# Decode attention of two models on one core: a scheduler that prices tiling switches and issue time, K of B in 32 KB packets, more places for K

## The chip, the cores and the metric

The kernel runs on one core of a Trainium2 chip. The metric is the device time of one execution in microseconds (us), lower is better. Engines in the profile: PE is the matrix engine, PEld its weight loads, DVE the vector engine, ACT the scalar engine, POOL the general engine, SP (SyncE) the one that issues all DMA transfers here; SPq is its queue. Sixteen DMA engines carry each transfer together: each of the 498 transfers of the kernel leaves 16 completion packets of 4 bytes in the trace. A *place* or *slot* is a buffer in the on-chip memory that holds one load. *Landing* is the moment when a load is complete.

## The reference

Two attention layers with given K and V caches, computed side by side; the outputs are joined on the last axis.

```python
# A: B=16 sequences, 32 new tokens each, D=1024, 32 query heads, 4 K/V heads, 1024 cached positions, head size 128
# B: the same, but with 32 K/V heads
q = (x @ wq).reshape(B, Sq, 32, 128).transpose(0, 2, 1, 3)
scores = einsum("bhqd,bhkd->bhqk", q, k) * 128 ** -0.5      # k, v of A repeated 8 times over heads
p = softmax(scores)
o = einsum("bhqk,bhkd->bhqd", p, v)
out = o.transpose(0, 2, 1, 3).reshape(B, Sq, 4096) @ wo
# result: concatenate([out_A, out_B], axis=-1), everything in bf16
```

B's caches are eight times A's: K and V of B are 268 MB of the 338 MB that the kernel reads. There is little arithmetic per byte, so the transfers matter most.

## The kernel before

The program is written as a list of operations, each with the buffers that it reads and writes. A list scheduler with a small time model then fixes the order of the instructions on each engine, and semaphore waits are derived from the buffers. The work is cut into 128 steps. A step of B handles four heads of one sequence: 1 MB of K, 1 MB of V.

```python
NVB_SLOTS = 3          # places for V of B
NKB_SLOTS = 2          # places for K of B
SP_AHEAD = 1.5         # how far SyncE's issues may run ahead of the modelled DMA stream, us
PE_MODE = {"scoresB": 2, "PVB": 1}
MODE_SWITCH = 0.11     # one price for each change of PE's tiling
...
QB_sb = sb("QB_sb", [P, 3, 4, NTOK], BF)           # Q of B, three places
KB_sb = sb("KB_sb", [P, NKB, 2, 16 * Dh], BF)      # K of B as it is loaded
ost = sb("ost", [P, 2, D], BF)                     # staging of the output
...
# scheduler: an issue on SyncE costs 0.06 us, a transfer its bytes / 390 GB/s, then 1.8 us to landing
free[op.eng] = st + 0.06
xs = max(st + 0.06, dma_free[0])
dma_free[0] = xs + op.dur / dma_bw
op.t1 = dma_free[0] + dma_lat
...
# most loads: 32 reads of one contiguous stretch, each written over four partitions
def wide_load(e, dst, src, groups=32):
    inst = mybir.InstDMACopy(..., ins=e.lower_ap_dma(src.rearrange("(g n) d -> g (n d)", g=groups)), outs=e.lower_ap_dma(dst))
...
# K of B: 128 partitions of 8 KB each, an ordinary load: 128 packets of 8 KB
ksrc = pb["k"][q.b, q.h0:q.h0 + 4].rearrange("a (p s) d -> (a p) (s d)", s=32)
e.dma_start(KB_sb[:, sl, :, :].rearrange("p i n -> p (i n)"), ksrc)
...
# a step of B
st_ktrB(q, 0); st_ktrB(q, 1)              # DVE transposes K in 32 x 32 blocks; the place is free after it
if t + NKB < NIT: st_dmaK(quadsB[t + NKB])
if t >= 1 and t - 1 + NVB < NIT: st_dmaV(quadsB[t - 1 + NVB])
st_scores(q); st_exp(q); st_ptr(q); st_pev(q, "act"); st_pv(q); st_recip(q); st_norm(q, "dve"); st_otr(q, "act")
```

## Time and profile before

| | before |
|---|---|
| time, median of the first 3 runs | 844.96 us (844.0 to 846.38) |
| span of the profiled run | 843.8 us |
| DMA queue of the loads, share of 16 engines | 98.4% |
| PE, DVE, ACT busy | 84%, 66%, 53% |

The first lines of the profile's page of the kernel before, and its DMA part. In the row of tenths each digit is the busy share of one fortieth of the span; GB/s is what moved in it.

```profile
PE 707.7 (84%) x11977; PEld 431.9 (51%) x12104; DVE 553.2 (66%) x1117; ACT 448.3 (53%) x981; POOL 68.1 (8%) x76
...
DMA  9999999999999999999999999999999999999994
GB/s 343 377 412 376 419 418 412 418 421 417 404 415 416 418 420 417 408 403 416 416 419 418 418 419 421 421 405 420 407 409 416 419 419 421 402 404 416 411 405 172
DMA packets 56726, 341.52 MB, mean 405 GB/s; under 512 B 7968, under 2 KB 8480, under 8 KB 17440
...
q1 hardware_dynamic: 56608, 339.77, 98.4%
q8 instruction: 95, 1.56, 0.7%
...
DMA 52%; PE 27%; DVE 15%; SPq 2%; issue 2%; ACT 1%; POOL 1%; DVEq 0%; POOLq 0%
```

Three things say the same: the DMA row is full until the last slice, the load queue (q1) was busy for 98.4% of the span, and over half of the chain that ended last is DMA. q8 are fetches of instructions, which the page counts on the same 16 engines.

What held SyncE's queue before its issues, in the kernel before (who waited, for whom, us in total, times, longest). L825 issues K of B, L514 V of B, L499 everything that goes through the wide load, A's K and V above all.

```profile
SPq L825 <- DVE KBt_sb L859: 139.0, 38, 8.2
SPq L499 <- POOL VAp_sb L834: 82.6, 33, 6.4
SPq L825 <- DVE stat L922: 77.6, 30, 7.5
SPq L825 <- DVE OB_sb L1002: 73.2, 20, 6.3
SPq L514 <- PE ps_o L986: 30.5, 16, 7.9
```

All waits of L825 together are 364 of SyncE's 522 us of waiting. SyncE stands before K of B until DVE has emptied a place.

### The profile page before, as it was taken

The page shows a single profiled execution, that of the slowest core. Times are in us where ns is not written, and L with a number is a line of the kernel's source. Part 1 is how long each engine was busy: PE and PEld are TensorE (multiplying, and loading weights), DVE is VectorE, ACT ScalarE, POOL GpSimd, SP SyncE. Part 2 cuts the span into 40 slices and gives each one's busy share as a digit, 9 for nine tenths or more (in the row PEclk, how much of TensorE's full clock was granted, in tenths as well). Part 3 has the DMA queues.
Part 4 walks back from the last instruction along what each step waited for, and adds up shares of the span by engine and source line. Part 5 has one row for each costly group of instructions (what it writes and reads, how often), then busy time and mean ns, then how long its engine had stood idle before and what let it go on. Part 6 is the DMA issues. An engine that isn't in the chain of part 4 may idle for free.

```text
span 843.8 us, 27217 instructions
## 1 busy us (share of the span) xinstructions
PE 707.7 (84%) x11977; PEld 431.9 (51%) x12104; DVE 553.2 (66%) x1117; ACT 448.3 (53%) x981; POOL 68.1 (8%) x76
## 2 busy tenths in 40 slices
PE   3999999799978798788987879987999867887876
PEld 2555665456545465455554435554565534554543
DVE  0654666566855687567775758774778856757764
ACT  1455666566645465445654545554565634645562
POOL 0000000000001000010000000000000000000000
PEclk9999999999999999999999989999999999999999
DMA  9999999999999999999999999999999999999994
GB/s 343 377 412 376 419 418 412 418 421 417 404 415 416 418 420 417 408 403 416 416 419 418 418 419 421 421 405 420 407 409 416 419 419 421 402 404 416 411 405 172
DMA packets 56726, 341.52 MB, mean 405 GB/s; under 512 B 7968, under 2 KB 8480, under 8 KB 17440
## 3 DMA queue, kind: packets, MB, share of 16 engines
q1 hardware_dynamic: 56608, 339.77, 98.4%
q8 instruction: 95, 1.56, 0.7%
q14 instruction: 23, 0.19, 0.1%
HBM read 337.64 MB, written 2.10 MB: 403 GB/s over the span
## 4 chain that ended last, share of the span: by engine, by line
DMA 52%; PE 27%; DVE 15%; SPq 2%; issue 2%; ACT 1%; POOL 1%; DVEq 0%; POOLq 0%
DMA KB_sb<-in_B_k_cache_dram 33%; DVE KBt_sb L859 12%; PE ps_pj L690 7%; DMA VA_sb<-in_A_v_cache_dram 6%; PE ps_s L894 4%; PE ps_pj L747 4%; DMA VB_sb<-in_B_v_cache_dram 4%; DMA wq_sb<-in_B_wq_dram 3%; PE ps_kt L952 3%; DMA woB_sb<-in_B_wo_dram 2%; PE ps_o L986 2%; DMA wq_sb<-in_A_wq_dram 2%; PE ps_pt L936 2%; PE ps_s L877 2%; DMA acc<-in_B_x_dram 1%
## 5 line engine op out<-in xcount | busy, mean ns | idle before, releaser
L859 DVE STREAM_TRANSPOSE KBt_sb<-KB_sb 128x1024 f32<-128x1024 f32 x256 | 304.9, 1224 | 73.6 <-DMA KB_sb<-in_B_k_cache_dram 64.6
L917 ACT ACTIVATE P_sb<-ps_s 128x512 bf16<-128x512 f32 x256 | 151.4, 597 | 81.4 <-PE ps_s L894 67.7
L909 ACT ACTIVATE PTA_sb<-ps_s 128x1024 bf16<-128x1024 f32 x128 | 131.3, 1026 | 88.1 <-PE ps_s L877 62.2
L894 PE MATMUL ps_s<-KBt_sb,QB_sb 32*32 32x512 bf16 x4096 | 141.5, 383 | 11.8 <-DVE KBt_sb L859 8.8
L620 ACT COPY PT_sb<-ps_pt 128x512 f32<-128x512 f32 x128 | 75.0, 586 | 114.8 <-PE ps_o L986 88.3
L834 POOL COPY VAp_sb<-VA_sb 128x1024 bf16<-128x1024 bf16 x64 | 66.6, 1041 | 758.0 <-DMA VA_sb<-in_A_v_cache_dram 703.7
L690 PE MATMUL ps_pj<-xT_sb,wq_sb 128*128 128x512 bf16 x401 | 112.0, 388 | 12.7 <-DMA wq_sb<-in_B_wq_dram 3.8
L936 PE MATMUL ps_pt<-id,P_sb 128*128 128x128 f32 x512 | 103.1, 303 | 15.2 <-ACT P_sb L917 12.0
L986 PE MATMUL ps_o<-VB_sb,PT_sb 128*32 128x128 bf16 x4096 | 82.0, 223 | 30.3 <-DMA VB_sb<-in_B_v_cache_dram 29.4
L936 PEld LDWEIGHTS ps_pt<-id,P_sb 128*128 128x128 f32 x512 | 81.5, 205 | 40.1 <-ACT P_sb L917 21.7
L986 PEld LDWEIGHTS ps_o<-VB_sb,PT_sb 128*32 128x32 bf16 x4096 | 59.4, 97 | 67.5 <-DMA VB_sb<-in_B_v_cache_dram 44.0
L877 PE MATMUL ps_s<-QT_sb,KTA_sb 128*128 128x256 bf16 x512 | 84.3, 274 | 10.9 <-ACT PTA_sb L909 5.6
L952 PE MATMUL ps_kt<-VAp_sb,PTA_sb 128*128 128x129 bf16 x1024 | 74.3, 220 | 9.0 <-POOL VAp_sb L834 5.3
L894 PEld LDWEIGHTS ps_s<-KBt_sb,QB_sb 32*32 32x32 bf16 x4096 | 48.6, 88 | 64.6 <-DVE KBt_sb L859 14.4
L952 PEld LDWEIGHTS ps_kt<-VAp_sb,PTA_sb 128*128 128x128 bf16 x1024 | 63.4, 97 | 30.4 <-POOL VAp_sb L834 12.3
L1002 DVE TENSOR_SCALAR OB_sb<-ps_o,rinv_all 128x128 bf16<-128x128 f32 x128 | 43.6, 341 | 50.1 <-PE ps_o L986 48.9
L922 DVE TENSOR_TENSOR stat<-stat 64x1 f32<-64x1 f32 x256 | 50.7, 198 | 25.4 <-ACT P_sb L917 17.6
L747 PE MATMUL ps_pj<-woB_sb,OTB_sb 128*128 128x512 bf16 x195 | 56.5, 382 | 8.9 <-DMA woB_sb<-in_B_wo_dram 4.8
L690 PEld LDWEIGHTS ps_pj<-xT_sb,wq_sb 128*128 128x128 bf16 x448 | 41.2, 108 | 43.1 <-DMA wq_sb<-in_B_wq_dram 5.8
L877 PEld LDWEIGHTS ps_s<-QT_sb,KTA_sb 128*128 128x128 bf16 x512 | 44.3, 98 | 36.2 <-ACT PTA_sb L909 10.4
L747 PE MATMUL ps_pj<-woA_sb,OTA_sb 128*128 128x512 bf16 x200 | 54.6, 392 | 7.0 <-DMA woA_sb<-in_A_wo_dram 2.7
L758 DVE TENSOR_TENSOR acc<-acc,ps_pj 128x512 f32<-128x512 f32 x64 | 43.1, 673 | 18.4 <-PE ps_pj L747 17.3
(52 smaller groups left out, 518.8 us busy)
## 6 DMA issues: line engine op xcount, KB each, us to landing
KB_sb<-in_B_k_cache_dram SPq DMA_DIRECT2D x128, 1024.0 KB, 8.7
KA_sb<-in_A_k_cache_dram SPq DMA_DIRECT2D x64, 256.0 KB, 10.1
VA_sb<-in_A_v_cache_dram SPq DMA_DIRECT2D x64, 256.0 KB
wq_sb<-in_B_wq_dram SPq DMA_DIRECT2D x16, 512.0 KB, 11.2
woB_sb<-in_B_wo_dram SPq DMA_DIRECT2D x32, 256.0 KB, 10.2
woA_sb<-in_A_wo_dram SPq DMA_DIRECT2D x32, 256.0 KB, 8.8
wq_sb<-in_A_wq_dram SPq DMA_DIRECT2D x12, 512.0 KB, 11.4
woA_sb<-in_A_wq_dram SPq DMA_DIRECT2D x4, 512.0 KB, 8.9
```

Of the source, the lines that this page charges most:

```text
L620: pr.add("act", lambda e: e.copy(dst_ap, src_ap), reads=reads, writes=writes, name=name + "@act", wtag=wtag, rtag=rtag)
L690: last = e.matmul(ps_pj[:, 0:NTOK], pick(src, j), xT_sb[:, pi, j, :], start=(j == 0), stop=(j == DJ - 1))
L747: last = e.matmul(ps_a[:, 0:OUTW], OT[:, gp, hh, :], wo_[:, hh, oh * OUTW:(oh + 1) * OUTW], start=(hh == 0), stop=(hh == nh - 1))
L834: pr.add("pool", lambda g: g.tensor_copy(VAp_sb[:, sl, :, 0:Dh], VA_sb[:, :, :]), reads=["VA"], writes=[("VAp", sl)], name="VAp_cp", rtag= ...
L859: pr.add("dve", lambda e: e.transpose(KBt_sb[:, sl, t_, :].bitcast(F32).rearrange("p (s r i) -> p s r i", r=2, i=32), KB_sb[:, rs, t_, :]. ...
L877: last = e.matmul(ps_s[:, sbf, c2, i * 2 * P:(i + 1) * 2 * P], KTA_sb[:, sl, c * P:(c + 1) * P], qt, start=True, stop=True)
L894: last = e.matmul(ps_s[32 * cg:32 * cg + 32, sbf, g, :].rearrange("p (sh cl j) -> p sh cl j", sh=4, cl=4), lhsT, kt[32 * a:32 * a + 32, g, ...
L909: pr.add("act", lambda e: e.activation(dst, src, ACTF.Exp, scale=scale), writes=BK_S[sbf] + [("PTA", q.half)], name="expA", rtag={("Sv", s ...
L917: pr.add("act", lambda e, src=src, dst=dst, g=g: e.activation(dst, src, ACTF.Exp, scale=scale, accum_out=st[:, g:g + 1]), writes=[BK_S[sbf ...
L936: last = e.transpose(ps_pt32[:, m * P:(m + 1) * P], p32[:, m:Sk // 2:NPK], id32[:])
L952: last = e.matmul(ps_kt[:, qh * OA0:qh * OA0 + Dh + 1], PTA_sb[:, h, c, qh * P:(qh + 1) * P], VAp_sb[:, sl, 4 * h + c, 0:Dh + 1], start=(h ...
L986: last = e.matmul(ps_o[32 * a:32 * a + 32, 0:Dh], PT_pairs[:, c // 2, 32 * (a ^ (c // 4 * 2)):32 * (a ^ (c // 4 * 2)) + 32, c % 2], VB_sb[ ...
```

## The change

The intent: give the scheduler finer costs (a switch of PE's tiling by its kind, an issue on SyncE 0.5 to 0.75 us in place of 0.06, a transfer by its number and size of packets; in the trace before, issues of loads have medians of 0.33 us for K of B to 0.72 us for V of B), take K of B in larger packets, and give K more places, so that loads are issued earlier. The larger packets come with another form of load: K of B, an ordinary load before, now goes through the wide load, whose reads are each written over four partitions. The third place for K is paid by one place of Q of B and by staging the output in a free half of A's Q. Late in the kernel, when the query weights and x are no longer needed, their room gives four more.

```diff
-NKB_SLOTS = 2
+NKB_SLOTS = 3
-DMA_BW = 390e3
-SP_AHEAD = 1.5
-PE_MODE = {"scoresB": 2, "PVB": 1}
-MODE_SWITCH = 0.11
+BONUS = {...}                    # per kind of operation, cut
+SWITCH_WEIGHT = 2.619
+PIECE = {"kb_dma": (32768, 32), "wq_dma": (2048, 256), "vb_dma": (8192, 128), "out_dma": (2048, 128)}
+SP_COST = {"kb_dma": 0.66, "vb_dma": 0.75, "wq_dma": 0.5, "out_dma": 0.5}
+SP_AHEAD = 3.904
+PE_LEAVE = {"S": 0.35, "V": 0.16, "F": 0.0}
+PE_ENTER = 0.22
 ... (durations of the operations measured anew, cut)
-                free[op.eng] = st + 0.06
-                xs = max(st + 0.06, dma_free[0])
-                dma_free[0] = xs + op.dur / dma_bw
+                free[op.eng] = st + SP_COST.get(op.name, SP_COST_DEFAULT)
+                dma_free[0] = max(free[op.eng] + DMA_START, dma_free[0]) + self.transfer(op)
 ... (cut)
-        QB_sb = sb("QB_sb", [P, 3, 4, NTOK], BF)
+        QB_sb = sb("QB_sb", [P, 2, 4, NTOK], BF)
-        ost = sb("ost", [P, 2, D], BF)
+        ost = QT_sb[:, NSB % 2, 0:2 * D // (HS * Sq), :, :].rearrange(...)
+        LATE = 3 * NIT // 4 + 8
+        spare = [... two halves of wq_sb, two of xT_sb ...]
+        k_places = [(KB_sb[:, i, :, :].rearrange("p i n -> p (i n)"), []) for i in range(NKB)] + spare
-                pr.add("sp", lambda e: e.dma_start(KB_sb[:, sl, :, :].rearrange("p i n -> p (i n)"), ksrc), ...)
+                pr.add("sp", lambda e: wide_load(e, place, ksrc), ...)
-            if t + NKB < NIT:
+            if t + NKB < LATE:
                 st_dmaK(quadsB[t + NKB])
+            elif t + NKB + NSP < NIT:
+                st_dmaK(quadsB[t + NKB + NSP])
 ... (the projections of Q of B at later steps, cut)
```

More of the change, by code (lines that the diff above doesn't have):

```diff
@@ L20 @@
 A_STEPS_FRAC = 1.0
-DMA_BW = 390e3
-SP_STRICT = False
-SP_AHEAD = 1.5
-DMA_MARGIN = {}
-DMA_MARGIN_DEFAULT = 1.0
-PRIO_BONUS = {}
-PE_MODE = {"scoresB": 2, "PVB": 1}
-MODE_SWITCH = 0.11
-DUR = {
-    "scoresB": 0.222, "scoresA": 0.222, "PT_trB": 0.235, "PVA": 0.312, "PVB": 0.116, "OT_tr": 0.08, "OT_trA": 0.16,
-    "KTA_tr": 0.62, "qprojA": 0.434, "qprojB": 0.434, "oprojA": 0.434, "oprojB": 0.434, "xT_tr": 0.62, "exp": 0.8, "expA": 1.03,
-    "PT_ev@act": 0.587, "OT_ev@act": 0.27, "OT_evA@dve": 0.3, "KTA_ev@act": 1.01, "KTA_ev@dve": 0.685, "qA_ev@act": 0.59,
-    "qA_ev@dve": 0.69, "qB_ev@act": 0.59, "qB_ev@dve": 0.69, "acc0": 0.59, "acc+": 0.68, "accF": 0.68, "xT_ev@act": 1.01,
-    "xT_ev@dve": 0.69, "KBt_tr": 1.23, "recip": 0.15, "shift": 0.165, "norm@dve": 0.347, "normA@dve": 0.4, "VAp_cp": 1.04,
-    "c0": 0.2, "c1": 0.3,
+LOOK = 0.005
@@ new lines @@
+A_LEAD = 69.16
+BONUS = {
+    "KTA_ev@act": 6.5, "KTA_ev@dve": -19.9, "KTA_tr": 1.6, "OT_ev@act": 2.7, "OT_tr": 2.8, "OT_trA": -1.0, "PT_ev@act":
+    9.6, "PT_trB": 0.4, "PVA": -4.9, "PVB": 13.7, "acc+": 3.4, "exp": 9.0, "expA": -3.4, "ka_dma": 0.5, "kb_dma": 6.2,
+    "norm@dve": 6.2, "oprojA": 5.0, "oprojB": -0.7, "qprojA": 5.9, "qprojB": 0.6, "scoresA": 1.0, "scoresB": -28.4,
+    "woA_dma": 1.6, "woB_dma": 5.5, "wq_dma": 0.1,
+}
+SWITCH_WEIGHT = 2.619
+DMA_MARGIN = 1.417
+PIECE = {"kb_dma": (32768, 32), "wq_dma": (2048, 256), "vb_dma": (8192, 128), "out_dma": (2048, 128)}
@@ new lines @@
+PIECE_DEFAULT = (8192, 32)
+SP_COST = {"kb_dma": 0.66, "vb_dma": 0.75, "wq_dma": 0.5, "out_dma": 0.5}
+SP_COST_DEFAULT = 0.63
+DMA_START = 1.7
+SP_AHEAD = 3.904
+DMA_LAND = 0.5
+DMA_SLOW = 1.0
+PE_CLASS = {"scoresB": "S", "PVB": "V"}
+PE_LEAVE = {"S": 0.35, "V": 0.16, "F": 0.0}
+PE_ENTER = 0.22
+PE_SLOW = 1.049
+SEEN = {"act": 0.16, "dve": 0.13, "pool": 0.05, "pe": 0.29, "sp": 0.04}
+DUR = {
+    "scoresB": 0.22, "scoresA": 0.232, "PT_trB": 0.23, "PVA": 0.229, "PVB": 0.105, "OT_tr": 0.06, "OT_trA": 0.11, "KTA_tr": 0.456,
+    "qprojA": 0.432, "qprojB": 0.432, "oprojA": 0.432, "oprojB": 0.432, "xT_tr": 0.8,
+    "exp": 0.586, "expA": 0.911, "PT_ev@act": 0.47, "OT_ev@act": 0.157, "KTA_ev@act": 0.908, "qA_ev@act": 0.48, "qB_ev@act": 0.48,
+    "acc0": 0.48, "xT_ev@act": 0.9,
+    "KBt_tr": 1.127, "KTA_ev@dve": 0.58, "OT_evA@dve": 0.18, "qA_ev@dve": 0.6, "qB_ev@dve": 0.6, "acc+": 0.58, "accF": 0.59,
+    "xT_ev@dve": 0.6, "recip": 0.07, "shift": 0.1, "norm@dve": 0.23, "normA@dve": 0.31, "check": 0.3, "flag": 0.1,
+    "VAp_cp": 1.04, "c0": 0.1, "c1": 0.2,
@@ L164, in finalize, with transfer, list_schedule @@
             op.clock = clk
-    def simulate(self, lat=0.2, dma_bw=DMA_BW, dma_lat=1.8, jitter=0.0, seed=0):
-        rstate = [seed * 2654435761 % 2147483647 + 1]
-        def uni(a_, b_):
-            rstate[0] = (rstate[0] * 48271) % 2147483647
-            return a_ + (b_ - a_) * (rstate[0] / 2147483647.0)
-        free = {}
-        dma_free = 0.0
-        pe_mode = 0
-        for op in self.ops:
-            ready = 0.0
-            for d in op.deps:
-                if d.dma_key is None and d.eng == op.eng and op.eng == "pe":
-                    continue
-                if d.t1 + lat > ready:
-                    ready = d.t1 + lat
-            st = max(ready, free.get(op.eng, 0.0))
-            jf = 1.0 + (uni(-jitter, jitter) if jitter else 0.0)
-            if op.eng == "pe":
-                m = PE_MODE.get(op.name, 0)
-                if m != pe_mode:
-                    st += MODE_SWITCH
-                pe_mode = m
-            if op.dma_key is not None:
-                free[op.eng] = st + 0.06
-                xs = max(st + 0.06, dma_free)
-                dma_free = xs + jf * op.dur / dma_bw
-                op.t0 = st
-                op.t1 = dma_free + dma_lat
-            else:
-                op.t0 = st
-                op.t1 = st + op.dur * jf
-                free[op.eng] = op.t1
-        return max(op.t1 for op in self.ops)
-    def list_schedule(self, lat=0.2, dma_bw=DMA_BW, dma_lat=1.8, look=0.1):
+    @staticmethod
+    def transfer(op):
+        size, n = PIECE.get(op.name, PIECE_DEFAULT)
+        return (n / 16 * (0.009 + size / 27300.0) + 0.009) * DMA_SLOW
+    def list_schedule(self):
         ops = self.ops
@@ L209, in list_schedule, with length @@
                 users[d.idx].append(op.idx)
-        def odur(op):
+        def length(op):
             if op.dma_key is not None:
-                return 0.06 + op.dur / dma_bw + dma_lat
-            return op.dur
+                return DMA_START + self.transfer(op) + DMA_LAND
+            return op.dur + SEEN[op.eng]
         bl = [0.0] * n
         for i in range(n - 1, -1, -1):
-            m = 0.0
-            for u in users[i]:
-                v = bl[u] + lat
-                if v > m:
-                    m = v
-            bl[i] = odur(ops[i]) + m + ops[i].prio + PRIO_BONUS.get(ops[i].name.split("@")[0], 0.0)
+            bl[i] = length(ops[i]) + max([bl[u] for u in users[i]], default=0.0) + ops[i].prio
         ready_t = [0.0] * n
@@ L229, in list_schedule @@
         order = []
-        pe_mode = [0]
-        sp_order = [i for i in range(n) if ops[i].eng == "sp"]
-        sp_pos = [0]
+        mode = ["F"]
         dma_free = [0.0]
@@ L237, in sw, with toll @@
                 return 0.0
-            return MODE_SWITCH if PE_MODE.get(ops[i].name, 0) != pe_mode[0] else 0.0
+            c = PE_CLASS.get(ops[i].name, "F")
+            if c == mode[0]:
+                return 0.0
+            return PE_LEAVE[mode[0]] + (PE_ENTER if mode[0] == "F" else 0.0)
+        def toll(i):
+            if ops[i].eng != "pe":
+                return 0.0
+            c = PE_CLASS.get(ops[i].name, "F")
+            if c == mode[0] or c == "F":
+                return 0.0
+            return PE_LEAVE[c] + (PE_ENTER if mode[0] == "F" else 0.0)
         while True:
@@ L247, in list_schedule @@
                     fe = max(fe, dma_free[0] - SP_AHEAD)
-                if eng == "sp" and SP_STRICT:
-                    ci = sp_order[sp_pos[0]]
-                    if ci not in lst:
-                        continue
-                    st = max(ready_t[ci], fe)
-                    key = (st, -bl[ci])
-                    if bkey is None or key < bkey:
-                        bkey = key
-                        best = ci
-                    continue
-                emin = min(max(ready_t[i], fe) + sw(i) for i in lst)
-                cand = [i for i in lst if max(ready_t[i], fe) + sw(i) <= emin + look]
-                ci = max(cand, key=lambda i: (bl[i] - 8.0 * sw(i), -i))
-                st = max(ready_t[ci], fe) + sw(ci)
-                key = (st, -bl[ci])
+                at = {i: max(ready_t[i], fe + sw(i)) for i in lst}
+                emin = min(at.values())
+                ci = max([i for i in lst if at[i] <= emin + LOOK], key=lambda i: (bl[i] + BONUS.get(ops[i].name, 0.0) - SWITCH_WEIGHT * toll(i), -i))
+                key = (at[ci], -bl[ci])
                 if bkey is None or key < bkey:
@@ L269, in list_schedule @@
             ready[op.eng].remove(best)
-            if op.eng == "sp":
-                sp_pos[0] += 1
-            st = max(ready_t[best], free.get(op.eng, 0.0)) + sw(best)
+            st = max(ready_t[best], free.get(op.eng, 0.0) + sw(best))
             if op.eng == "sp":
                 st = max(st, dma_free[0] - SP_AHEAD)
-            if op.eng == "pe":
-                pe_mode[0] = PE_MODE.get(op.name, 0)
             op.t0 = st
             if op.dma_key is not None:
-                free[op.eng] = st + 0.06
-                xs = max(st + 0.06, dma_free[0])
-                dma_free[0] = xs + op.dur / dma_bw
-                op.t1 = dma_free[0] + dma_lat
-            else:
-                op.t1 = st + op.dur
+                free[op.eng] = st + SP_COST.get(op.name, SP_COST_DEFAULT)
+                dma_free[0] = max(free[op.eng] + DMA_START, dma_free[0]) + self.transfer(op)
+                op.t1 = dma_free[0] + DMA_LAND
+                seen = op.t1
+            else:
+                dur = op.dur
+                if op.eng == "pe":
+                    mode[0] = PE_CLASS.get(op.name, "F")
+                    dur *= PE_SLOW
+                op.t1 = st + dur
                 free[op.eng] = op.t1
+                seen = op.t1 + SEEN[op.eng]
             order.append(best)
@@ L288, in list_schedule @@
                 uo = ops[u]
-                same_pe = (op.dma_key is None and op.eng == uo.eng and uo.eng == "pe")
-                r = op.t1 + (0.0 if same_pe else lat)
+                r = op.t1 if op.eng == uo.eng == "pe" else seen
                 if uo.dma_key is not None:
-                    r += DMA_MARGIN.get(uo.name, DMA_MARGIN_DEFAULT)
+                    r += DMA_MARGIN
                 if r > ready_t[u]:
@@ L304, in list_schedule @@
         return newp
-    def report(self, a, b, engs=("pe", "act", "dve", "sp")):
-        col = {e: i for i, e in enumerate(engs)}
-        last = {}
-        for op in sorted(self.ops, key=lambda o: o.t0):
-            if op.eng not in col or op.t0 < a or op.t0 > b:
-                continue
-            gap = op.t0 - last.get(op.eng, op.t0)
-            last[op.eng] = op.t1 if op.dma_key is None else op.t0 + 0.06
-            print("%9.2f %-4s %s%-10s %5.2f gap=%5.2f %s" % (op.t0, op.eng, " " * (22 * col[op.eng]), op.name[:10], op.t1 - op.t0, gap, op.tag or ""))
-    def busy(self):
-        b = {}
-        for op in self.ops:
-            if op.dma_key is None:
-                b[op.eng] = b.get(op.eng, 0.0) + op.dur
-            else:
-                b["dma"] = b.get("dma", 0.0) + op.dur / 385e3
-        return b
     def sem_names(self):
@@ L589, in build @@
         OB_sb = sb("OB_sb", [P, Dh], BF)
-        ost = sb("ost", [P, 2, D], BF)
+        ost = QT_sb[:, NSB % 2, 0:2 * D // (HS * Sq), :, :].rearrange("p b h q -> p (b h q)").rearrange("p (u d) -> p u d", u=2)
+        ost_space = [("QT", NSB % 2, h_) for h_ in range(HS)]
         zeros = PT_sb[:, 0, :]
@@ L628, in xT_stage @@
                 pr.add("sp", lambda e, tc=tc: wide_load(e, xst[:, tc, :], xfs[pi][tc * P:(tc + 1) * P, :]),
-                       writes=accres if tc == 0 else [("xst", pi, tc)], reads=[] if tc == 0 else accres, dma_key=f"x{pi}_{tc}", name="x_dma", dur=P * D * 2)
+                       writes=accres if tc == 0 else [("xst", pi, tc)], reads=[] if tc == 0 else accres, dma_key=f"x{pi}_{tc}", name="x_dma")
             for tc in range(NG):
@@ L641, in xT_stage, with ost_claim @@
                     evac(xT_sb[:, pi, j0:j0 + jn, tc * P:(tc + 1) * P], ps_pt[:, 0:jn * P].rearrange("p (j t) -> p j t", j=jn),
-                         reads=[BK_PT], writes=[BK_PT, ("xT", pi, tc)], name="xT_ev")
+                         reads=[BK_PT], writes=[BK_PT, ("xT", pi, tc)], name="xT_ev", wtag={("xT", pi, tc): "x"})
+        ost_free = [False]
+        def ost_claim():
+            first = not ost_free[0]
+            ost_free[0] = True
+            return dict(reads=[], writes=ost_space) if first else dict(reads=ost_space, writes=[])
         lazy = []
@@ L679, in th @@
                                                        wq[k_ * jp * P:(k_ + 1) * jp * P, c * WQC:(c + 1) * WQC].rearrange("(j p) c -> p j c", p=P)),
-                           writes=keys, dma_key=f"wq{k_}" if key(0)[0] == "wq" else f"wqa{k_}", name="wq_dma", dur=jp * P * WQC * 2,
+                           writes=keys, dma_key=f"wq{k_}" if key(0)[0] == "wq" else f"wqa{k_}", name="wq_dma",
                            wtag={k: ("wq", pi, c) for k in keys})
@@ L692, in qproj_piece @@
             keys = sorted({key(j) for j in range(j0, j0 + JS)})
-            pr.add("pe", e_qp, reads=keys + [("xT", pi, t) for t in range(NG)], writes=[BK_PJ], name="qprojA" if pi == 0 else "qprojB",
-                   dur=0.217 * JS, rtag={k: ("wq", pi, c) for k in keys})
+            pr.add("pe", e_qp, reads=keys + [("xT", pi, t) for t in range(NG)], writes=[BK_PJ], name="qprojA" if pi == 0 else "qprojB", rtag=dict([(k, ("wq", pi, c)) for k in keys] + [(("xT", pi, t), "x") for t in range(NG)]))
         def qprojA_head(s_, hh):
@@ L707, in qprojB @@
                 qproj_piece(1, m_ // 2, lambda w, j: w[:, j, c0 + fp:c0 + CW:4], NTOK, j0, 2)
-            evac(QB_sb[:, m_ % 3, fp, :], ps_pj[:, 0:NTOK], reads=[BK_PJ], writes=[BK_PJ, ("QB", m_ % 3, fp)], name="qB_ev",
-                 wtag={("QB", m_ % 3, fp): m_})
+            evac(QB_sb[:, m_ % 2, fp, :], ps_pj[:, 0:NTOK], reads=[BK_PJ], writes=[BK_PJ, ("QB", m_ % 2, fp)], name="qB_ev",
+                 wtag={("QB", m_ % 2, fp): m_})
         def wo_loadA(s_):
@@ L717, in th @@
                     pr.add("sp", lambda e: wide_load(e, woA_sb[:, h_, :], wo[r0:r0 + Dh, :]),
-                           writes=[("woA", h_)], dma_key=f"woA{h_}", name="woA_dma", dur=Dh * D * 2, wtag={("woA", h_): s_})
+                           writes=[("woA", h_)], dma_key=f"woA{h_}", name="woA_dma", wtag={("woA", h_): s_})
                 lazy_push(("wo", 0, s_), th)
@@ L727, in th @@
                     pr.add("sp", lambda e: wide_load(e, woB_sb[:, h_, :], wo[r0:r0 + Dh, :]),
-                           writes=[("woB", h_)], dma_key=f"woB{h_}", name="woB_dma", dur=Dh * D * 2, wtag={("woB", h_): m_})
+                           writes=[("woB", h_)], dma_key=f"woB{h_}", name="woB_dma", wtag={("woB", h_): m_})
                 lazy_push(("wo", 1, m_), th)
@@ L750, in oproj @@
                     pr.add("pe", e_op, reads=[("OT", pi, gp, h0_), ("OT", pi, gp, h0_ + 1), (wo_res, h0_), (wo_res, h0_ + 1)], writes=[bk],
-                           name="oprojA" if pi == 0 else "oprojB",
-                           dur=0.434 * OUTW / 512, rtag={(wo_res, h0_): blk, (wo_res, h0_ + 1): blk, ("OTv", pi, gp): (blk, G)})
+                           name="oprojA" if pi == 0 else "oprojB", rtag={(wo_res, h0_): blk, (wo_res, h0_ + 1): blk, ("OTv", pi, gp): (blk, G)})
                 a_ap = acc[:, pi, G, oh * OUTW:(oh + 1) * OUTW]
@@ L760, in oproj @@
                 else:
+                    claim = ost_claim()
                     pr.add("dve", lambda e, a_ap=a_ap, o_ap=o_ap, ps_a=ps_a: e.tensor_tensor(o_ap, a_ap, ps_a[:, 0:OUTW], ALU.add),
-                           reads=[bk, ("acc", pi, G, oh)], writes=[bk, ("ost", ob, oh)], name="accF")
+                           reads=[bk, ("acc", pi, G, oh)] + claim["reads"], writes=[bk, ("ost", ob, oh)] + claim["writes"], name="accF", prio=A_LEAD if pi == 0 else 0.0)
                     if G == NG - 1:
@@ L765, in oproj @@
                                                                   ost[:, ob, oh * OUTW:(oh + 1) * OUTW]),
-                               reads=[("ost", ob, oh)], dma_key=f"out{ob}_{oh}", name="out_dma", dur=P * OUTW * 2)
+                               reads=[("ost", ob, oh)], dma_key=f"out{ob}_{oh}", name="out_dma")
             if final and G < NG - 1:
                 pr.add("sp", lambda e: e.dma_start(out_flat[G * P:(G + 1) * P, cols[pi]:cols[pi] + D], ost[:, ob, :]),
-                       reads=[("ost", ob, oh) for oh in range(NOH)], dma_key=f"out{ob}", name="out_dma", dur=P * D * 2)
+                       reads=[("ost", ob, oh) for oh in range(NOH)], dma_key=f"out{ob}", name="out_dma")
         class Quad:
@@ L792, in mk_quadA, with k_slot @@
             return q
+        LATE = 3 * NIT // 4 + 8
+        spare = [(wq_sb[:, :, :].rearrange("p j c -> p (j c)")[:, i * DJ * WQC // 2:(i + 1) * DJ * WQC // 2],
+                  [("wq", k_) for k_ in range(i * WQP // 2, (i + 1) * WQP // 2)]) for i in range(2)]
+        spare += [(xT_sb[:, i, :, :].rearrange("p j t -> p (j t)"), [("xT", i, tc) for tc in range(NG)]) for i in range(2)]
+        NSP = len(spare)
+        k_places = [(KB_sb[:, i, :, :].rearrange("p i n -> p (i n)"), []) for i in range(NKB)] + spare
+        def k_slot(t):
+            if t < LATE:
+                return t % NKB
+            i = (t - LATE) % (NKB + NSP)
+            return NKB + i if i < NSP else (LATE + i - NSP) % NKB
         def mk_quadB(t):
@@ L803, in mk_quadB @@
             q.kvslot = t % 2
-            q.krslot = t % NKB
+            q.krslot = k_slot(t)
             q.vslot = t % NVB
@@ L820, in st_dmaK @@
                 pr.add("sp", lambda e: wide_load(e, KA_sb[:, sl, :, :].rearrange("p c d -> p (c d)"), pa["k"][q.b, q.s]),
-                       writes=[("KA", sl)], dma_key=f"ka{sl}", name="ka_dma", dur=Sk * Dh * 2, wtag={("KA", sl): q.kid})
+                       writes=[("KA", sl)], dma_key=f"ka{sl}", name="ka_dma", wtag={("KA", sl): q.kid})
             else:
                 sl = q.krslot
+                place, keys = k_places[sl]
                 ksrc = pb["k"][q.b, q.h0:q.h0 + 4].rearrange("a (p s) d -> (a p) (s d)", s=32)
-                pr.add("sp", lambda e: e.dma_start(KB_sb[:, sl, :, :].rearrange("p i n -> p (i n)"), ksrc), writes=[("KB", sl)], dma_key=f"kb{sl}", name="kb_dma", dur=4 * Sk * Dh * 2, wtag={("KB", sl): q.kid})
+                pr.add("sp", lambda e: wide_load(e, place, ksrc), writes=[("KB", sl)] + keys, dma_key=f"kb{sl}", name="kb_dma", wtag=dict([(("KB", sl), q.kid)] + [(k_, None) for k_ in keys]))
         def st_dmaV(q):
@@ L832, in st_dmaV @@
                 pr.add("sp", lambda e: wide_load(e, VA_sb[:, :, :].rearrange("p c d -> p (c d)"), pa["v"][q.b, q.s]),
-                       writes=["VA"], dma_key="va", name="va_dma", dur=Sk * Dh * 2, wtag={"VA": q.kid})
+                       writes=["VA"], dma_key="va", name="va_dma", wtag={"VA": q.kid})
                 pr.add("pool", lambda g: g.tensor_copy(VAp_sb[:, sl, :, 0:Dh], VA_sb[:, :, :]), reads=["VA"], writes=[("VAp", sl)], name="VAp_cp",
@@ L839, in st_dmaV @@
                 pr.add("sp", lambda e: wide_load_slots(e, VB_sb[:, sl, :, :, :].rearrange("p a c d -> p a (c d)"), vsrc), writes=[("VB", sl)],
-                       dma_key=f"vb{sl}", name="vb_dma", dur=4 * Sk * Dh * 2, wtag={("VB", sl): q.kid})
+                       dma_key=f"vb{sl}", name="vb_dma", wtag={("VB", sl): q.kid})
         def st_ktrA(q):
@@ L859, in st_ktrB @@
             pr.add("dve", lambda e: e.transpose(KBt_sb[:, sl, t_, :].bitcast(F32).rearrange("p (s r i) -> p s r i", r=2, i=32),
-                                                   KB_sb[:, rs, t_, :].bitcast(F32).rearrange("p (s i r) -> p s r i", r=2, i=32)),
+                                                   k_places[rs][0][:, t_ * 16 * Dh:(t_ + 1) * 16 * Dh].bitcast(F32).rearrange("p (s i r) -> p s r i", r=2, i=32)),
                    reads=[("KB", rs)], writes=[("KBt", sl, t_)], name="KBt_tr", rtag={("KB", rs): q.kid}, wtag={("KBt", sl, t_): q.kid})
@@ L878, in e_st @@
                         return last
-                    pr.add("pe", e_st, reads=[("QT", q.s % 2, a) for a in range(HS)] + [("KTA", sl)], writes=BK_S[sbf], name="scoresA", dur=0.222,
+                    pr.add("pe", e_st, reads=[("QT", q.s % 2, a) for a in range(HS)] + [("KTA", sl)], writes=BK_S[sbf], name="scoresA",
                            tag="A%d" % q.t, rtag=dict([(("QT", q.s % 2, a), q.s) for a in range(HS)] + [(("KTA", sl), q.kid)]),
@@ L890, in e_s @@
                     for a in range(4):
-                        lhsT = QB_sb[32 * a:32 * a + 32, q.m % 3, fp, q.b * Sq:(q.b + 1) * Sq]
+                        lhsT = QB_sb[32 * a:32 * a + 32, q.m % 2, fp, q.b * Sq:(q.b + 1) * Sq]
                         for g in range(2):
@@ L898, in st_scores @@
                 for fp_ in range(4):
-                    pr.add("pe", lambda e, fp_=fp_: e_s(e, fp_), reads=[("QB", q.m % 3, fp_), ("KBt", sl, 0), ("KBt", sl, 1)],
-                           writes=BK_S[sbf], name="scoresB", dur=0.222, tag="B%d" % q.t,
-                           rtag={("QB", q.m % 3, fp_): q.m, ("KBt", sl, 0): q.kid, ("KBt", sl, 1): q.kid},
+                    pr.add("pe", lambda e, fp_=fp_: e_s(e, fp_), reads=[("QB", q.m % 2, fp_), ("KBt", sl, 0), ("KBt", sl, 1)],
+                           writes=BK_S[sbf], name="scoresB", tag="B%d" % q.t,
+                           rtag={("QB", q.m % 2, fp_): q.m, ("KBt", sl, 0): q.kid, ("KBt", sl, 1): q.kid},
                            wtag={("Sv", sbf): q.qid})
@@ L937, in e_pt @@
                     return last
-                pr.add("pe", e_pt, reads=[("P", g), "id32"], writes=[BK_PT], name="PT_trB", dur=0.235, rtag={("P", g): q.qid}, wtag={"PTps": q.qid})
+                pr.add("pe", e_pt, reads=[("P", g), "id32"], writes=[BK_PT], name="PT_trB", rtag={("P", g): q.qid}, wtag={"PTps": q.qid})
         def st_pev(q, eng="act"):
@@ L955, in st_pvA @@
             for c0 in (0, 2):
-                pr.add("pe", lambda e, c0=c0: e_pv(e, c0), reads=[("PTA", h), ("VAp", sl)], writes=[BK_KT], name="PVA", dur=0.312, tag="A%d" % q.t,
+                pr.add("pe", lambda e, c0=c0: e_pv(e, c0), reads=[("PTA", h), ("VAp", sl)], writes=[BK_KT], name="PVA", tag="A%d" % q.t,
                        rtag={("PTA", h): q.qid, ("VAp", sl): q.kid}, wtag={"OpsA": q.kid})
@@ L989, in st_pv @@
             for c0 in range(0, NCH, 2):
-                pr.add("pe", lambda e, c0=c0: e_pv(e, c0), reads=["PT", ("VB", kvs)], writes=[BK_O], name="PVB",
-                       dur=0.116, tag="B%d" % q.t, rtag={"PT": q.qid, ("VB", kvs): q.kid}, wtag={"Ops": q.qid})
+                pr.add("pe", lambda e, c0=c0: e_pv(e, c0), reads=["PT", ("VB", kvs)], writes=[BK_O], name="PVB", tag="B%d" % q.t, rtag={"PT": q.qid, ("VB", kvs): q.kid}, wtag={"Ops": q.qid})
         def st_recip(q):
@@ L1128, in build @@
         for s_ in range(NSB):
-            if s_ == 0:
-                for fp in range(4):
-                    proj.setdefault(fp, []).append((1, 1, fp))
+            for k_ in range(4):
+                proj.setdefault(s_ * PER + k_, []).append((1, 2 * s_ + 1, k_))
             if s_ + 1 < NSB:
-                a0 = 5 if s_ == 0 else 1
                 for k_ in range(HS):
-                    proj.setdefault(s_ * PER + a0 + (3 * k_) // 2, []).append((0, s_ + 1, k_))
-                    proj.setdefault(s_ * PER + 18 + (3 * k_) // 2, []).append((1, 2 * (s_ + 1) + k_ // 4, k_ % 4))
+                    proj.setdefault(s_ * PER + 8 + (3 * k_) // 2, []).append((0, s_ + 1, k_))
+                for k_ in range(4):
+                    proj.setdefault(s_ * PER + 23 + 2 * k_, []).append((1, 2 * s_ + 2, k_))
         order_of_chunks = [(1, 0)] + [x for s_ in range(1, NSB) for x in ((0, s_), (1, s_))]
@@ L1161, in build @@
             lazy_pop(LAZY_PER_STEP)
+            if t == LATE - NSP:
+                for u in range(NSP):
+                    st_dmaK(quadsB[LATE + u])
             if t == NIT - NLATE:
```

## The prediction

> **What bounds it now.** The load stream. The page's DMA row is 9 in all slices but the last; the queue table gives the load queue 98.4% of 16 engines' span; 341.5 MB go at a mean of 405 GB/s, 416-421 in most slices. The DMA packet records show loads without a pause from 2.1 to about 830 us. PE is busy 84%, DVE 66%, ACT 53%. The chain of waits is half DMA (52%), mostly K of B (33%). So the time is start (2 us) + load stream (828 us) + tail (about 13 us).
>
> In the packet records an 8 KB packet takes 309 ns (some 315), a 2 KB packet 84 ns: 9 ns per packet plus 27.3 bytes/ns. The Trainium skill, "DMA: Bandwidth & Descriptors", section "Bandwidth", puts the ceiling of the fabric at 435 GB/s and names a fixed cost per packet; this trace agrees: 16 x 8192 B / 309 ns = 424 GB/s.
>
> **What the change does.**
>
> 1. K of B (128 loads of 1 MB): 128 packets of 8 KB become 32 of 32 KB. Estimate: 1209 ns in place of 4 x 309 = 1236. 4096 packets x 27 ns / 16 engines = 6.9 us less, all on the stream, if a 32 KB packet written over four partitions is not slower (A's K, 8 KB over four partitions, shows no penalty: 309-315).
>
> 2. Three K slots in place of two, four more late (in the room of the query weights and x), SyncE allowed to run 3.9 us in place of 1.5 ahead, real issue costs in the scheduler. Now SyncE waits long for DVE to free K (the queue's waits: some 360 us ahead of K loads), with little queued. The cost is small, since the stream is rarely dry: missing engine time outside start and end is 4 us, and 8 KB packets far over 309 ns (404 of them over 0.5 us) add about 12 us, part of which is instruction fetch that stays. I expect 6-9 of these 16 us back.
>
> 3. Scheduler weights for PE tiling modes: fewer switches (2588 runs of instructions on PE against 2702). PE is not the bound; nothing by itself.
>
> 4. B's Q in two slots, output staging in Q of A: room for the third K slot; Q projections come nearer their use. A small risk of waits.
>
> 5. Tail: the order still has A's last projection (4 us) ahead of the last PV of B. I expect 0-3 us.
>
> Sum: 7 + 7.5 + 1.5, about 16-17 us.
>
> **Predicted: 828 us**, 8 in 10 between 819 and 838. Faster by over 2% (under 828.4): 0.50; within 2%: 0.48; slower: 0.02.
>
> **What would show it.** Step 1: some 12,000 fewer DMA packets, a full slice at 424-430 GB/s where it was 416-421. Step 2: fewer long packets, no dips (366, 395, 402 GB/s in 20 us windows before), DVE's wait for K loads (64.6 us) much shorter. Step 3: PE busy time the same to 2%. Step 5: from last load landed to the end 10-13 us.
>
> **What would make it wrong.** 32 KB packets costing 1236 ns or more (then about 835); compute now late instead of loads, since PE has little slack in its first 140 us (19 of 20 us busy); long packets caused by something other than an empty queue (then 832-835); or dips vanishing wholly and a shorter tail (then 818).

## More of the kernel before

The place of K, and how long a load took from its issue to its landing, in the kernel before (the last lines of the view of the tile KB_sb):

```profile
who waited for it (us, times):
  DVE KBt_sb L859: 64.6, 67
...
DMA to landing us min/median/max: 6.2/8.7/15.1
```

1 MB at 424 GB/s is 2.5 us. A load has a fixed part too: the four 128 KB stores at the end of the kernel took 1.8 us each, where 128 KB at that rate is 0.3 us. So a load of K with nothing in front of it would take about 4 us (an estimate from these two). Even the fastest took 6.2 us: other transfers stood in front of it.

Add up the bytes of all transfers that SyncE has issued, and subtract the bytes that packets have moved by then. From 20 to 815 us the kernel before had 2.6 MB outstanding at the median, and less than 1 MB for only 10.4 of the 795 us. It did come close to empty, at 39 us for about a microsecond (least value 0.03 MB), but hardly ever. (The count is over all 16 engines; the packed trace doesn't say which one a packet ran on.)

## The result, and the profile after

| | before | after |
|---|---|---|
| time, median of 4 runs each | 844.48 us (842.72 to 846.38) | 836.94 us (836.62 to 838.18) |
| ratio | | 0.9913 [0.9889, 0.9938]: the same within 2% |
| span of the profiled run | 843.8 us | 834.8 us |

The ratio is the mean time of one kernel's fast runs over that of the other's of the same rounds, so not quite the ratio of the two medians. The gain is 7.5 us, clear of the noise, where 16 to 17 had been forecast.

The same lines of the page, of the kernel after:

```profile
PE 727.4 (87%) x12104; PEld 436.5 (52%) x12104; DVE 548.9 (66%) x1117; ACT 452.0 (54%) x981; POOL 68.2 (8%) x76
...
DMA  9999999999999999999999999999999999999995
GB/s 353 437 404 420 431 411 422 413 414 422 420 413 419 412 426 403 425 417 416 406 423 406 419 417 416 413 422 416 419 413 413 410 423 427 413 385 426 405 411 205
DMA packets 44441, 341.55 MB, mean 409 GB/s; under 512 B 7968, under 2 KB 8480, under 8 KB 17440
...
q1 hardware_dynamic: 44320, 339.77, 98.8%
q8 instruction: 96, 1.57, 0.7%
...
DMA 47%; PE 31%; DVE 10%; SPq 4%; issue 4%; ACT 3%; POOL 2%; POOLq 0%; DVEq 0%
```

The kernel has 12,288 fewer load packets, the same bytes, and the load queue is as full as before. Single slices show 437 and 431 GB/s, but this view counts a packet's bytes in the slice where it starts, and a packet is now 32 KB; spread over the packet's time, the same slices moved 425 and 420. Others still dip (385, 403, 405), and the mean rises only from 405 to 409. The 727 us of PE beside 708 must not be read as more work: both kernels run the same 12,104 matmuls, and the trace before lacks 127 of their records (11,977).

SyncE's queue in the kernel after. L459 now issues everything that goes through the wide load, K of B as well; L474 is V of B:

```profile
SPq L459 <- POOL VAp_sb L815: 150.5, 46, 6.3
SPq L474 <- PE ps_o L967: 104.9, 49, 7.0
SPq L459 <- DVE stat L903: 80.7, 34, 6.0
SPq L459 <- DVE KBt_sb L840: 46.7, 18, 7.6
```

The waits for DVE's transposes of K fell from 139 to 47 us. In their place SyncE stands before A's V (its one place is free when POOL has copied it: 82.6 became 150.5) and before V of B (30.5 became 104.9). The sum over all waits of SyncE hardly moved: 522 us before, 494 after.

The tile KB_sb in the kernel after:

```profile
who waited for it (us, times):
  DVE KBt_sb L840: 41.4, 34
...
DMA to landing us min/median/max: 8.6/10.8/22.6
```

These are 113 of the 128 loads of K. The other 15 go to the four late places and are listed under the buffers whose room they use (number, KB each, median us to landing):

```profile
wq_sb<-in_B_k_cache_dram SPq DMA_DIRECT2D x8, 1024.0 KB, 12.5
xT_sb<-in_B_k_cache_dram SPq DMA_DIRECT2D x7, 1024.0 KB, 15.7
```

The loads of K are issued earlier: they land 10.8 us or more after the issue in place of 8.7, and DVE waits 43 us for them in place of 65 (41.4, and 1.6 for a load in a late place). By the count of outstanding bytes, the queue held 3.0 MB at the median and never less than 0.88 MB from 20 to 815 us. The places do what they were meant for. It is only worth little.

**Where the 9 us between the two profiled runs lie.** The times of all DMA packets are in the trace. From the first load packet to the last one landed is the load stream; for each packet size the shortest common time is taken as its nominal time (309 ns for 8 KB, 84 ns for 2 KB, 9 ns for a completion; 1209 ns for 32 KB is the value on the line through the first two, and not a time that was measured). A packet counts as long when it took over 0.15 us more than that. All are us of one engine, that is the sum over all packets divided by 16.

| us | before | after | difference |
|---|---|---|---|
| from the span's start to the first load packet | 2.1 | 2.1 | 0 |
| load stream | 829.1 | 823.1 | -6.0 |
| from the last load landed to the end | 12.6 | 9.6 | -3.0 |
| **span** | **843.8** | **834.8** | **-9.0** |
| of the stream: packets at their nominal times | 807.8 | 801.0 | -6.8 |
| fetches of instructions | 5.9 | 5.9 | 0 |
| small excess over nominal (under 0.15 us each) | 7.6 | 10.4 | +2.8 |
| excess of long packets | 13.0 | 11.8 | -1.2 |
| idle time less overlap of packets | -5.6 | -6.5 | -0.9 |

The last row is negative because packets overlap in the records: at times more than 16 are open at once, which comes to 11.1 us before and 9.3 after. The time in which fewer than 16 are open, the idle time by itself, is 5.5 us before and 2.8 after (at least: where records overlap, an idle engine does not show). So the change did take away idle time, 2.7 us of it, but the overlap shrank as well.
The rows of the stream add up to its length within half a microsecond; a few records at its ends are not split.

Some windows of 20 us of both kernels (start and end, length, then busy us of PE, PEld, DVE, ACT and POOL with counts, PE's granted clock, DMA share, GB/s). Before:

```profile
60.00:80.00 20.00, 18.54 (x211) 11.95 (x213) 10.41 (x21) 11.25 (x18) 2.08 (x2) 1.00 0.98 366
140.00:160.00 20.00, 17.45 (x354) 10.26 (x342) 10.54 (x29) 12.61 (x32) 1.04 (x1) 1.00 1.02 416
200.00:220.00 20.00, 18.41 (x360) 11.99 (x360) 14.38 (x32) 13.04 (x28) 3.00 (x3) 1.00 1.01 415
720.00:740.00 20.00, 17.03 (x305) 10.26 (x308) 14.44 (x31) 11.29 (x26) 1.04 (x1) 1.00 1.00 395
740.00:760.00 20.00, 15.85 (x317) 10.32 (x322) 11.87 (x28) 9.76 (x23) 2.08 (x2) 0.91 1.01 411
```

After:

```profile
60.00:80.00 20.00, 19.96 (x271) 12.92 (x270) 10.52 (x23) 12.41 (x24) 2.09 (x2) 0.98 1.01 415
140.00:160.00 20.00, 18.61 (x310) 11.42 (x308) 11.00 (x24) 12.12 (x24) 3.13 (x3) 1.00 0.99 393
200.00:220.00 20.00, 19.12 (x363) 11.57 (x365) 15.38 (x32) 13.73 (x29) 2.10 (x2) 1.00 1.03 429
720.00:740.00 20.00, 14.66 (x325) 7.69 (x324) 15.96 (x31) 9.28 (x25) 0.00 (x0) 1.00 1.00 414
740.00:760.00 20.00, 16.34 (x253) 9.55 (x252) 8.34 (x22) 9.31 (x20) 2.10 (x2) 0.84 1.01 395
```

The dip of 366 GB/s is gone, one of 395 has moved by a window, and a new one of 393 has come. The best window shows 429; spread over the packets' time, it is 420, the new dip is 403, and no stretch of 20 us in either kernel, by steps of 1 us, is over 426. The DMA share is 0.98 to 1.03 in all of them, dips included: a low rate here is mostly not an idle engine but engines busy at a lower rate, with smaller packets (16 x 2048 B / 84 ns is only 390 GB/s) or with long ones. The steps of the two kernels do not lie at the same times, so windows may not be subtracted from each other.

The two ends of the kernels in the chain of waits, in order of time (start, length, what). Before:

```profile
825.79 1.06 PE ps_s L894 x26
...
829.79 1.30 issue
...
832.27 0.63 PE ps_pj L747
```

After:

```profile
822.88 0.66 PE ps_o L967 x32
...
824.20 0.57 PE ps_pj L714 x2
```

L747 before and L714 after are the first matmul of A's last projection. Before, it starts 1.0 us after the last load has landed (832.27 against 831.23): a late score group of B and 1.3 us of nothing on the chain stand ahead of it. After, it starts 1.0 us before the last load has landed (824.20 against 825.24). That is 2 of the 3 us that the tail lost. (The times of landing are those of the packets.)

### The profile page after: what moved, and what is told of

It is laid out like the page before. It is cut to its first block, busy times and chain, and to the rows that moved or that the text cites. A ratio compares the mean times of both kernels' runs of the same rounds, so it can differ in the third digit from the quotient of the medians.

```text
span 834.8 us, 27414 instructions
## 1 busy us (share of the span) xinstructions
PE 727.4 (87%) x12104; PEld 436.5 (52%) x12104; DVE 548.9 (66%) x1117; ACT 452.0 (54%) x981; POOL 68.2 (8%) x76
## 3 DMA queue, kind: packets, MB, share of 16 engines
q1 hardware_dynamic: 44320, 339.77, 98.8%
## 4 chain that ended last, share of the span: by engine, by line
DMA 47%; PE 31%; DVE 10%; SPq 4%; issue 4%; ACT 3%; POOL 2%; POOLq 0%; DVEq 0%
DMA KB_sb<-in_B_k_cache_dram 20%; DMA VA_sb<-in_A_v_cache_dram 13%; DMA VB_sb<-in_B_v_cache_dram 7%; DVE KBt_sb L840 7%; PE ps_pj L658 7%; PE ps_pj L714 6%; PE ps_s L875 5%; DMA KA_sb<-in_A_k_cache_dram 3%; PE ps_o L967 3%; PE ps_pt L917 2%; PE ps_kt L933 2%; PE ps_s L858 2%; SPq L459 2%; DMA wq_sb<-in_B_wq_dram 2%; POOL VAp_sb L815 2%
## 5 line engine op out<-in xcount | busy, mean ns | idle before, releaser
L840 DVE STREAM_TRANSPOSE KBt_sb<-KB_sb 128x1024 f32<-128x1024 f32 x226 | 273.9, 1230 | 81.5 <-DMA KB_sb<-in_B_k_cache_dram 41.4
L658 PE MATMUL ps_pj<-xT_sb,wq_sb 128*128 128x512 bf16 x448 | 115.1, 388 | 6.4 <-DMA wq_sb<-in_B_wq_dram 3.1
L917 PE MATMUL ps_pt<-id,P_sb 128*128 128x128 f32 x512 | 104.9, 307 | 8.8 <-ACT P_sb L898 5.2
L917 PEld LDWEIGHTS ps_pt<-id,P_sb 128*128 128x128 f32 x512 | 79.3, 207 | 29.4 <-ACT P_sb L898 17.9
L933 PE MATMUL ps_kt<-VAp_sb,PTA_sb 128*128 128x129 bf16 x1024 | 77.0, 222 | 5.6 <-POOL VAp_sb L815 4.5
L933 PEld LDWEIGHTS ps_kt<-VAp_sb,PTA_sb 128*128 128x128 bf16 x1024 | 66.5, 99 | 16.9 <-POOL VAp_sb L815 8.0
L714 PE MATMUL ps_pj<-woB_sb,OTB_sb 128*128 128x512 bf16 x240 | 66.9, 392 | 3.0 <-DVE acc L724 2.0
L658 PEld LDWEIGHTS ps_pj<-xT_sb,wq_sb 128*128 128x128 bf16 x448 | 43.3, 109 | 49.2 <-issue 6.9
L903 DVE TENSOR_TENSOR stat<-stat 64x1 f32<-64x1 f32 x256 | 46.1, 180 | 27.3 <-ACT P_sb L898 19.6
L581 ACT COPY OTB_sb<-ps_o 128x128 bf16<-128x128 bf16 x128 | 34.5, 270 | 47.1 <-PE ps_o L987 46.1
L714 PE MATMUL ps_pj<-woA_sb,OTA_sb 128*128 128x512 bf16 x224 | 54.2, 380 | 4.4 <-DVE OTA_sb L583 1.8
## 6 DMA issues: line engine op xcount, KB each, us to landing
KB_sb<-in_B_k_cache_dram SPq DMA_DIRECT2D x113, 1024.0 KB, 10.8
KA_sb<-in_A_k_cache_dram SPq DMA_DIRECT2D x64, 256.0 KB, 10.8
woA_sb<-in_A_wo_dram SPq DMA_DIRECT2D x32, 256.0 KB, 11.9
```

What stands on the lines that cost most here:

```text
L581: pr.add("act", lambda e: e.copy(dst_ap, src_ap), reads=reads, writes=writes, name=name + "@act", wtag=wtag, rtag=rtag)
L658: last = e.matmul(ps_pj[:, 0:NTOK], pick(src, j), xT_sb[:, pi, j, :], start=(j == 0), stop=(j == DJ - 1))
L714: last = e.matmul(ps_a[:, 0:OUTW], OT[:, gp, hh, :], wo_[:, hh, oh * OUTW:(oh + 1) * OUTW], start=(hh == 0), stop=(hh == nh - 1))
L840: pr.add("dve", lambda e: e.transpose(KBt_sb[:, sl, t_, :].bitcast(F32).rearrange("p (s r i) -> p s r i", r=2, i=32), k_places[rs][0][:, t ...
L917: last = e.transpose(ps_pt32[:, m * P:(m + 1) * P], p32[:, m:Sk // 2:NPK], id32[:])
L933: last = e.matmul(ps_kt[:, qh * OA0:qh * OA0 + Dh + 1], PTA_sb[:, h, c, qh * P:(qh + 1) * P], VAp_sb[:, sl, 4 * h + c, 0:Dh + 1], start=(h ...
```

## The experiments

None of the experiments gave a result. The kernels below passed the checks before the chip, and were submitted 32 times in five hours under new labels (b4 7 times, a4 6, b4_k32 4, a4_k8 5, alone_k32 10), but no chip took any of them; the reason lay outside of the kernels. So **everything said here of causes rests on the two traces alone, and is an argument from records, not a test.** The experiments are told with what was expected of them, because the expectations say what would have decided the matter.

The two theories:

- **Theory S, the stream.** The load stream itself is the clock. It stood only a few us over its floor already, so more places could give only little, and what came off is packet time and the tail.
- **Theory L, late places.** The stream has much room below it. Places still come free too late: the third K slot moved SyncE's wait from K to V, and the gain of the slots was lost to these new waits.

V of B is fetched in the given kernels by a load whose write side is set by hand, a form that may not be built anew. So a base pair was needed first, in which a step fetches V of B by four ordinary loads:

```diff
-                pr.add("sp", lambda e: wide_load_slots(e, VB_sb[:, sl, :, :, :].rearrange("p a c d -> p a (c d)"), vsrc), writes=[("VB", sl)],
+                pr.add("sp", lambda e: [wide_load(e, VB_sb[:, sl, a, :, :].rearrange("p c d -> p (c d)"), pb["v"][q.b, q.h0 + a]) for a in range(4)],
+                       writes=[("VB", sl)],
```

The semaphore of a V place counts 64 a step in place of 16. The scheduler's costs are not touched by this edit, so the order of the instructions on PE should stay that of the kernels before and after; no run shows it.

**b4 and a4: the pair with V in four loads.** Expected of b4:

> A base for all further runs: the kernel before, with V of B fetched by four ordinary 256 KB loads per step in place of one 1 MB load whose write side is described by hand (that form may not be built anew). Same 8 KB packets, same instruction order on PE; 384 more issues on SyncE and 384 x 16 more completion packets of 9 ns, which is 3.5 us of each transfer engine's time. Both theories expect 844 + 3 to 5 us, so about 847 to 849. If it is over 860, the issue time on SyncE has become a limit and this base is useless.

and of a4:

> The changed kernel with the same four loads for V. Both theories expect about 840 (837 + 3.5), so 0.990 to 0.993 of b4. A difference to b4 under 4 us or over 12 us would mean that this pair does not carry the change.

Measured: nothing.

**b4_k32: the kernel before with large packets alone.** This edit, and the one of a4_k8, changes the form of the load together with the size of its packets, so the two could not have told these apart.

```diff
-                pr.add("sp", lambda e: e.dma_start(KB_sb[:, sl, :, :].rearrange("p i n -> p (i n)"), ksrc), ...)
+                pr.add("sp", lambda e: wide_load(e, KB_sb[:, sl, :, :].rearrange("p i n -> p (i n)"), ksrc), ...)
```

> b4 with one edit: K of B in 32 KB packets. Theory S (the load stream is the clock, so packet time comes off the whole time one to one): 4.5 to 7 us less than b4, which is most of the whole change. Theory L (memory places come free too late, so faster packets only wait longer): under 2 us less than b4.

Measured: nothing.

**a4_k8: the kernel after without large packets.**

```diff
-                pr.add("sp", lambda e: wide_load(e, place, ksrc), ...)
+                pr.add("sp", lambda e: e.dma_start(place, ksrc), ...)
```

> a4 with K of B in 8 KB packets again, all slots and the new scheduler kept. Theory S: 4.5 to 7 us more than a4, within 3 us of b4. Theory L, where the slots and the scheduler bring the gain: under 2 us more than a4.

Measured: nothing.

**alone_k32: the loads without the work.** After the scheduler has fixed the order, all operations but SyncE's are dropped; a load then waits only for the load before it in the same place. Its output is wrong, which doesn't matter for the time.

```diff
-        pr = pr.list_schedule()
+        pr = loads_alone(pr.list_schedule(), QT_sb[:, NSB % 2, 0:2 * D // (HS * Sq), :, :], flag, 4 * P)
```

> Wrong result on purpose: the changed kernel's transfers in its order (V of B in four loads per step), with nothing else running; a load waits only for the load before it in the same place. It measures the floor of the load stream. Theory S: the stream was bound by the transfers themselves, so the floor lies within 12 us of the kernel's stream (first load to last load landed): stream of 812 to 822 us. Theory L: late places cost the stream tens of us, so the floor is 800 us or less.

Measured: nothing. This is the run that is missed most: it would have given the floor of the stream as a number (with V in four loads).

Planned: the kernel after with two K slots and no late ones, with three and no late ones, with the scheduler of before, and with 16 KB packets in the 256 KB loads.

## Why the prediction was wrong

**The bound was read rightly.** The load stream is the clock in both kernels: 829.1 of 843.8 us before, 823.1 of 834.8 after, with the load queue at 98.4% and 98.8%.

**Step 1, larger packets: the mechanism was right, and part of it was given back.** The packet count fell by 12,288 on the load queue (56,608 to 44,320), as forecast. At nominal times the stream shrank by 6.8 us (forecast 6.9). But the 32 KB packets took 1219 ns (median), not 1209 as the estimate had it: 4096 x 10 ns / 16 is 2.5 us, nearly all of the 2.8 us by which the small excess grew. So the line through the 2 KB and 8 KB packets was too good for the long ones: 4 of the 6.9 us were left in the stream.

The 8 KB packets tell something about this too. Before, 24,384 of the 39,168 in the load queue took at most 311 ns; after, only 3,857 of 22,784, and most of the others 315. A part of this is not a slowdown: the ones that are gone, K of B's, were the fast ones. If packets are assigned to loads by the order of issue (the middle of each load, an approximate assignment), about 88% of the packets of K of B took at most 311 ns before, but only about 52% of A's K and 43% of V of B, which are written over four partitions. So the prediction's check that A's K "shows no penalty" did not hold fully even in the trace before. The rest is a slowdown: of the packets of V of B about 16% took at most 311 ns after. Whether packets are stretched (8 KB by 2%, 32 KB by 1%) because they are written over four partitions or because the stream is near its ceiling is open. An ordinary load of K beside the wide one, and the loads alone, would have been the tests.

The Trainium skill, page "DMA: Bandwidth & Descriptors", section "Where 436 GB/s comes from", puts the ceiling of the ports at 435 GB/s. The trace agrees with a ceiling near that: 16 x 32768 B / 1219 ns is 430 GB/s, and no stretch of 20 us of the kernel after moved over 426, counted over the packets' time. For K of B, 134 MB, the step from 424 to that ceiling is 8 us: an estimate, from the page's figure, of the most that larger packets of K could have been worth.

**Step 2, places and issues: this is the step that failed.** The prediction said "I expect 6-9 of these 16 us back". In the profiled pair the long packets lost 1.2 us and the idle time less overlap 0.9 us: about 2 us together, and about 4 if the idle time is counted by itself. (The pair differs by 9.0 us where the medians differ by 7.5, so a term of the pair can be off by a microsecond or two.) Two readings in that step were wrong:

1. *A waiting SyncE was taken for a stream with little queued.* The prediction wrote that SyncE waits "with little queued". The count of outstanding bytes says otherwise: less than 1 MB for only 10.4 of 795 us. The idle time, the "missing engine time" of the prediction, did come back: from 20 to 815 us it fell from 4.1 to 1.1 us, though only 1.0 of the 4.1 lay in moments with less than 1 MB outstanding.
2. *The long packets were taken for a sign of an empty queue.* They made up 12 of the 16 us. But before, of the 11.9 us of excess in long packets from 20 to 815 us, only 0.25 fell in moments with less than 1 MB outstanding; and after, with never less than 0.88 MB, 10.3 us are still there. So what makes a packet long is something other than too little queued. What it is stays open. Instruction fetches are a part at most: 4.5 of the 13.0 us before lie in packets that ran at the same time as a fetch, and 5.6 of the 11.8 after, but fetches shifted to random times would meet 2.7 and 2.9 us by chance, and the packed trace does not say which engine a packet ran on. The remainder is spread over the whole kernel, most of its packets 0.15 to 0.4 us too long.

The waits of SyncE moved rather than went: K's transposes 139 to 47 us, but A's V 82.6 to 150.5 and V of B 30.5 to 104.9. Theory L would say that this is where the gain was lost. The traces speak against it: with all these waits in it, the queue of the kernel after never held less than 0.88 MB, about 2 us of transfers, and the engines were idle for 1.1 us from 20 to 815 us. So late places can hardly have cost the stream tens of us. But without the run of the loads alone it is not shown how low the stream could go when the packets themselves run faster.

**Step 3, tiling switches:** forecast as nothing by itself. The traces show nothing against that. PE has records missing before, so its busy time (708 and 727 us) could not serve as the check that the prediction meant it to be.

**Step 4, Q of B in two places:** forecast as a small risk of waits. In the list of waits of the kernel after, the scores of B wait for Q of B for 0.2 us in all. The risk did not come true in the scores.

**Step 5, tail:** forecast 0 to 3 us, measured 3.0 (12.6 to 9.6): at the upper end. A's last projection starts before the last load has landed, where it started after it.

**The sum:** forecast 7 + 7.5 + 1.5; the profiled pair shows about 4 + 2 + 3 = 9.0. Over four runs each the gain is 7.5 us, less than that of the profiled pair, since the profiled run of before (845.65 us) is one of its slower ones. The term that was mis-sized is the second. The prediction listed this outcome among those that would make it wrong ("long packets caused by something other than an empty queue"), and priced it at 832 to 835 us; with the 2.8 us of small excess added, this is near the measured 837.

**Still open,** since no experiment ran: the floor of the load stream; what makes packets long, or stretches most of them by 1 to 2%; how much of the gain each part (packets, slots, scheduler) brings by itself; and whether the tail's 3 us come from the scheduler's order or from the earlier loads.

## What to carry to other kernels

When a DMA queue is full by the profile, a long wait of the issuing engine says nothing by itself: count the bytes that are issued and not yet moved. If there are always some, more buffers mostly lengthen the queue. Before you promise a gain from "stalls", look how much of the stream's excess happens while the queue is short; only of that can one be sure that a fuller queue takes it away (here 1.0 us of the idle time and 0.25 us of the long packets). And measure a larger packet in the form in which it will be written, rather than on a line through smaller ones. Then the gain is the packet time saved and what the last operations after the last load can give, and each should be costed by itself.

## What the Trainium skill lacked or had wrong

- "DMA: Bandwidth & Descriptors", section "Bandwidth": it has no service time for large packets of loads issued from SyncE. Here, with all 16 engines streaming: 2 KB 84 ns, 8 KB 309 to 315 ns, 32 KB 1219 ns (median); from the first two alone one expects 1209 ns.
- The same page, "Rules for kernel authors", asks for 1 MiB or more in one transfer for the best bandwidth. In a queue that hardly ever runs dry this case shows no loss from 256 KB loads: A's K, in 32 packets of 8 KB, has packets of mostly 309 to 315 ns, as V of B has, which comes in loads of 1 MB and is written over four partitions too.
- The same page, "Where 436 GB/s comes from", says that for transfers between HBM and SBUF the HBM side, about 358 GB/s, binds. On one core here the kernel reads and writes at 403 (before) and 407 GB/s (after) over its whole span. The page's section "Bandwidth" says itself that its higher single-core figures hold while the other core of the pair is idle, so it is the sentence without this condition that misleads.
- "Runtime: NRT & Kernel Launch", section "Instruction fetch mechanics", says that the sequencer fetches its code in blocks of 16 KiB through a DMA queue of its own, and that this is mostly hidden. The trace agrees on the size (95 fetches of 16,384 bytes by the page of before, 96 by that of after) and that they go through a queue of their own. The page lacks how long they occupy DMA engines that are full: one takes 1.0 us here (median), all together 5.9 us of each engine's time in both kernels. What they cost the loads is not shown: the records of fetches and of data packets overlap, so this time may not be added to the excess of the packets beside them.
